# Stacks of queries in two transfers, denominators in one, a margin for transfers in the plan, and another order of key tiles

## The chip, the core and the metric

The kernel runs on one core of a Trainium2 chip. Its engines work through queues of their own, in order, and wait for each other by semaphores: TensorE (PE, with its weight loads PEld), VectorE (DVE), ScalarE (ACT), GpSimd (POOL) and SyncE (SP), which here issues every DMA. The metric is the device time of one execution in microseconds; a kernel's time is the median of its runs.

## The reference

Input x is 2048 rows of 448 floats. After a layernorm, multi-query attention and a gated MLP run side by side, and both are added to x:

```python
x = A_x
xn = _layernorm(x, axis=-1)
q = (xn @ wq).reshape(B, S, 16, 28).transpose(0, 2, 1, 3)     # 16 heads
k, v = xn @ wk, xn @ wv                                        # one head of keys and values, 28 wide
p = softmax(einsum("bhqd,bkd->bhqk", q, k) * 28 ** -0.5)
attention = einsum("bhqk,bkd->bhqd", p, v).transpose(0, 2, 1, 3).reshape(B, S, 448) @ wo
mlp = (silu(xn @ w1) * (xn @ w3)) @ w2                         # 448 -> 1792 -> 448
out = x + attention + mlp
```

(The projections, the softmax and the sum are written out from the reference's functions.) Everything is float32.

## The kernel before

**Work.** Queries are taken in 4 chunks of 512 (`qc`), heads 16 per chunk, so there are 64 steps `h`, in the text called heads. Float32 products are made from rounded parts: an operand is split into a high part and a low rest, and high x high, high x low and low x high are summed.

**Attention of one head.** `stack_load(h)` loads the head's queries into a stack `qs` of 84 rows (28 each of high, low and high) from a DRAM copy `qd`; the keys `kst` have three blocks that answer them. `leads(h)` makes 16 score tiles `ld` (128 keys x 512 queries each), one matmul each; VectorE keeps a running maximum `mx` over them. Ten of the sixteen tiles are *kept*: ScalarE copies them, in pairs, to SBUF (`pa`); KEEP lists the first tile of each pair. Then VectorE folds the maximum over the keys into `nm`, SP stores it to DRAM (`md`), loads it into the 85th row of the stack (`qs<-md`) and loads it broadcast over 128 partitions (`mb`). `weights_of(h, kt)` makes the exponentials: for a kept pair GpSimd adds the (negated) maximum, `pa<-pa,mb`, and ScalarE takes the exponential; the six tiles that are not kept are scored again with the 85th row (`sc`) and ScalarE takes their exponential from PSUM into `pb`. `values(h, j)` sums the weights with the values into `av`, in groups of 16 matmul records that mix the first half of head h with the second half of head h-1. `pair_done` and `norm` collect four heads in `o`, send their denominators through DRAM (`l1`, `l2`), take reciprocals, load them broadcast to 32 rows a head (`lb`, four transfers), and VectorE multiplies (`o<-o,lb`); `out_project` multiplies with `wo`.

**MLP.** `gate_up` and `down` make the tiles `g`, `u` and `dn` of 14 blocks of 128 columns per chunk, spread among the heads as filler for TensorE. Their split weights are made in the first chunk, stored, and loaded again (`w<-w13s`, `w<-w2s`) in the others.

**The order.** Nothing runs in the order in which it is written. `Plan.op` records each instruction with a cost, a latency and a due time; `Plan.order()` then plays a list scheduler: at each moment each engine takes the ready instruction of least due time, if its buffers can be had (`can`, with the pools MOST and SPARE, and SOON, how far ahead of the first TensorE work left a buffer may be taken). What comes out is the fixed order of every queue. The due times come from T0, T, LEAD and SPAN:

```python
    def begin(h):
        return T0 + T / 2 * h
```

The numbers only set the order. On the chip each engine goes as fast as its waits allow.

Of the kernel before, what the change touches and what calls it, by code (L numbers as in the profile page):

```python
# [20 lines left out]
P = 128  # L21
TC = 512
NQ = S // TC
TT = TC // P
HG = 4
# [18 lines left out]
MDUE, MRUSH, MSTEP = 28.0, 8, 9.0  # L44
MEND = -6.37
RATE = 290.0
BACKLOG = 1306.01
BULK = ("w13", "w2", "x", "raw", "raw2", "acc")
SOON = {"pa": 15.0, "qs": 0, "acc": 12.7, "o": 0, "x": 28.7}
PAIRS = 36  # L50
PAGES = 96 - 2 * PAIRS
SLACK = 37.1
REST = 0.0
LOADING = 105.0
BANKS = 8
MOST = {"pa": 19, "x": 16, "acc": 4, "w13": 5, "w2": 6, "h": 4, "oh": 3, "wo": 3, "xt": 4, "xn": 4, "wq": 4,
        "qt": 5, "pb": 7, "raw": 5, "raw2": 1, "t": 2, "qs": 6, "m": 2, "mxt": 3, "mb": 3, "o": 2, "lb": 1,
        "xp": 14, "wr": 4, "kv": 3, "at": 5, "mi": 6, "av": 2, "qp": 4}
SPARE = {"x": 3, "acc": 4, "w13": 2, "w2": 3, "raw": 4, "raw2": 3, "qt": 0, "wo": 0, "qs": 2}

# [26 lines left out]
class Plan:  # L87
# [40 lines left out]
    def order(self):  # L128
# [23 lines left out]

        def can(o):
# [143 lines left out]
def build(ctx, tc, x, wq, wk, wv, wo, w1, w3, w2, out):  # L297
# [39 lines left out]
    def dma(size, fn, **k):  # L337
        return plan.op("SP", 520.0, fn, size=size, **k)
# [170 lines left out]
    def project(qc, g, prio):  # L509
# [198 lines left out]
    def stack_load(h):  # L708
        q = stacks[h] = page("qs", f"qs{h}", F32R)
        plan.base = begin(h) - LEAD - SPAN - 8.0  # L710
        qc, lo = h // H, h % H * DH
        for b, src in enumerate((0, 1, 0)):
            dma(DH * TC * 4, lambda b=b, src=src: nc.sync.dma_start(
                f32(q.ap)[b * DH:(b + 1) * DH], qd[qc][src, lo:lo + DH]),
                reads=[qdb[qc, g] for g, (a, z) in enumerate(QROWS) if a < lo + DH and z > lo], parts=[q])

    def leads(h):

        mx, q = page("m", f"mx{h}"), stacks[h]
        last = None  # L720
        for kt in range(KT):
            plan.base = begin(h) - LEAD - SPAN + SPAN * kt / KT
            m = bank("at", f"ld{h}_{kt}")
            keep = kt in KEEP or kt - 1 in KEEP
            if kt in KEEP:
                p = pair("pa", f"pa{h}_{kt}")
            if keep:
                pt[h, kt] = p, int(kt not in KEEP)
            last = pe(512, lambda m=m, kt=kt: nc.tensor.matmul(  # L729
# [3 lines left out]
            if keep:  # L733
                act(512, lambda m=m, p=p, i=int(kt not in KEEP): nc.scalar.activation(p.ap[:, i], m.ap, AF.Copy),  # L734
                    reads=[m], parts=[p])
            if kt == 1:
                vec(512, lambda m=m, p=p: nc.vector.tensor_max(mx.ap, m.ap, p.ap[:, 0]), reads=[m], writes=[mx],
                    after=p.writers[:1], also=[p])
            elif kt:
                vec(512, lambda m=m: nc.vector.tensor_max(mx.ap, m.ap, mx.ap), reads=[m], writes=[mx])  # L740
# [27 lines left out]

    def weights_of(h, kt):


        plan.base = begin(h) + T * kt / KT
        if kt in KEEP:
# [14 lines left out]
    def values(h, j):  # L788


        todo = []
        for i in range(AVK):
            for g, kt in ((h, AVK * j + i), (h - 1, KT // 2 + AVK * j + i)):
                if 0 <= g < NH:
                    if g // 2 not in avb:
                        avb[g // 2] = bank("av", f"av{g // 2}")
                    todo.append((avb[g // 2], g, kt, *pt[g, kt]))

        def fn():
            for a, g, kt, p, i in todo:  # L800
                r = 64 * (kt % 2) + 32 * (g % 2)
                nc.tensor.matmul(a.ap[r:r + 32], vst_ap[:, kt], p.ap if i is None else p.ap[:, i], start=(kt < 2), stop=(kt >= KT - 2),  # L802
                                 skip_group_check=True)
        cost = AVK / 2 * 894.0 + 205.0
        plan.base = begin(h) + T * AVK * (j + 1) / KT + 1.5
        av_last[0] = plan.op("PE", cost, fn, lat=cost + 160.0,
                             reads=[p for *_, p, _ in todo] + [vst[kt // TT] for _, _, kt, _, _ in todo],
                             parts=[a for a, *_ in todo], after=[av_last[0]])

    def pair_done(u):  # L810
        w, half = divmod(u, 2)
        plan.base = begin(2 * u + 3) + 2.0
        if half == 0:
# [4 lines left out]
        vec(512, lambda: nc.vector.tensor_add(o.ap[r], a.ap[64:128], o.ap[r]), reads=[a], parts=[o],  # L818
            after=[c1])
        if half:  # L820
# [11 lines left out]
    def norm(w):  # L832
# [13 lines left out]
        lb = page("lb", f"lb{w}")  # L846
        for h in range(HG):
            dma(32 * TC * 4, lambda h=h: nc.sync.dma_start(
                lb.ap[32 * h:32 * h + 32], l2[h:h + 1].broadcast_to([32, TC])), reads=[l2b], parts=[lb])
        vec(512, lambda: nc.vector.tensor_mul(o.ap, o.ap, lb.ap), reads=[lb], writes=[o], cost=1000.0)  # L850
# [102 lines left out]
```

## Time and profile before

| | |
|---|---|
| median of 3 runs | 1169.39 us (1168.66 to 1171.07) |
| the profiled execution | 1164.6 us, span 1162.8 us |
| TensorE busy | 1130.5 us (97%), granted clock 0.996 |
| VectorE, ScalarE, GpSimd busy | 956.2, 961.4, 921.8 us |
| DMA queue | 101888 packets, 45.3% of the 16 engines' span |

A row of the page's groups gives line, engine, operation, out<-in, shape, count, busy time, mean of one, and the idle time before them with what ended it. A row of the waits gives who waited for whom, the total, the number and the longest. A piece of the chain gives start and length. `SPq` is SP's issuing.

### The profile page before, as it was taken

What the parts mean: (1) busy time and instruction counts of PE and PEld (TensorE: products, weight loads), DVE (VectorE), ACT (ScalarE), POOL (GpSimd) and SP (SyncE); (2) the same over time, 40 slices, a digit from 0 to 9 for tenths busy, and PEclk for the clock granted to TensorE, in tenths of its full rate; (3) what the DMA queues carried; (4) which work ended last, traced back from release to release, by engine and by line L of the source; (5) the groups of instructions that cost most, each with busy time, mean ns of one, the idle gap of its engine ahead of it and who ended that gap; (6) DMA issues with size and microseconds to landing.
All of it is one profiled execution on the core that took longest, in us unless ns stands there. A gap on an engine that the chain in (4) does not pass through costs nothing.

```text
span 1162.8 us, 18499 instructions
## 1 busy us (share of the span) xinstructions
PE 1130.5 (97%) x5810; PEld 742.1 (64%) x5810; DVE 956.2 (82%) x1798; ACT 961.4 (83%) x1599; POOL 921.8 (79%) x474
## 2 busy tenths in 40 slices
PE   6999999999999999999999999999999999999998
PEld 4876766565666666556666666566665666667664
DVE  7775688988798888888888888788898888898863
ACT  4546689999799988898899888898889888998873
POOL 4317899999688896888688878788788778988694
PEclk9999999999999999999999999999999999999998
DMA  7887874555513353232732551526243355143420
GB/s 201 274 300 246 279 244 140 186 191 187 180 47 103 102 195 117 89 120 68 237 127 65 160 183 33 152 60 194 67 171 101 109 165 172 62 132 108 145 61 32
DMA packets 101986, 168.68 MB, mean 145 GB/s; under 512 B 20980, under 2 KB 62644, under 8 KB 101888
## 3 DMA queue, kind: packets, MB, share of 16 engines
q1 hardware_dynamic: 101888, 167.50, 45.3%
q8 instruction: 46, 0.75, 0.3%
q14 instruction: 52, 0.43, 0.1%
HBM read 126.94 MB, written 39.83 MB: 143 GB/s over the span
## 4 chain that ended last, share of the span: by engine, by line
PE 52%; DVE 4%; ACT 3%; DMA 3%; issue 2%; POOL 1%; SPq 1%; DVEq 0%; ACTq 0%
PE av L802 13%; PE ld L729 12%; PE dn L361 7%; PE u L361 6%; PE g L361 6%; PE sc L782 5%; PE wo L361 3%; DVE mx L740 2%; DMA mb<-md 1%; ACT pa L734 1%; ACT pa L777 1%; DMA qs<-qd 1%; ACT pb L785 1%; POOL pa L775 1%; DMA lb<-l 1%
## 5 line engine op out<-in xcount | busy, mean ns | idle before, releaser
L775 POOL TENSOR_TENSOR pa<-pa,mb 128x1024 f32<-128x1024 f32 x320 | 761.8, 2412 | 107.3 <-DMA mb<-md 86.3
L740 DVE TENSOR_TENSOR mx<-ld,mx 128x512 f32<-128x512 f32 x896 | 583.0, 679 | 87.8 <-PE ld L729 64.0
L734 ACT ACTIVATE pa<-ld 128x512 f32<-128x512 f32 x640 | 369.0, 609 | 62.5 <-PE ld L729 53.4
L777 ACT ACTIVATE pa<-pa 128x1024 f32<-128x1024 f32 x320 | 343.5, 1077 | 30.3 <-POOL pa L775 30.1
L729 PE MATMUL ld<-qs,kst 84*128 84x512 f32 x1024 | 359.3, 409 | 9.0 <-DMA qs<-qd 3.1
L729 PEld LDWEIGHTS ld<-qs,kst 84*128 84x128 f32 x1024 | 188.3, 189 | 127.5 <-DVE mx L740 30.6
L785 ACT ACTIVATE pb<-sc 128x512 f32<-128x512 f32 x384 | 228.8, 611 | 27.1 <-PE sc L782 26.3
L802 PE MATMUL av<-pa,vst 128*32 128x512 f32 x1280 | 248.1, 600 | 0.3 <-DVE mx L740 0.2
L802 PE MATMUL av<-pb,vst 128*32 128x512 f32 x768 | 246.0, 596 | 0.0
L361 PE MATMUL dn<-w,h 128*128 128x448 f32 x672 | 171.1, 368 | 0.4 <-DVE o L818 0.3
L782 PE MATMUL sc<-qs,kst 85*128 85x512 f32 x384 | 154.6, 408 | 2.5 <-DVE acc L664 1.2
L361 PEld LDWEIGHTS dn<-w,h 128*128 128x128 f32 x672 | 126.1, 189 | 24.6 <-issue 5.5
L641 POOL TENSOR_TENSOR h<-t,h 128x512 fp32r<-128x512 f32 x56 | 72.6, 1296 | 54.9 <-ACT h L640 54.5
L802 PEld LDWEIGHTS av<-pa,vst 128*32 128x32 f32 x1280 | 51.5, 109 | 85.1 <-issue 71.6
L782 PEld LDWEIGHTS sc<-qs,kst 85*128 85x128 f32 x384 | 72.3, 188 | 41.5 <-issue 6.7
L802 PEld LDWEIGHTS av<-pb,vst 128*32 128x32 f32 x768 | 50.4, 109 | 38.6 <-issue 38.6
L664 DVE TENSOR_TENSOR acc<-dn,acc 128x448 f32<-128x448 f32 x80 | 48.8, 610 | 18.8 <-PE dn L361 18.3
L636 DVE SCALAR_TENSOR_TENSOR t<-u,t 128x512 f32<-128x512 f32 x56 | 38.2, 682 | 30.4 <-PE u L361 29.5
L361 PE MATMUL g<-x_0m,w 128*128 128x512 f32 x168 | 58.5, 398 | 0.3 <-DVE mx L740 0.3
L361 PE MATMUL u<-x_0m,w 128*128 128x512 f32 x168 | 56.4, 399 | 1.4 <-ACT pa L734 1.4
L361 PE MATMUL g<-x_2m,w 128*128 128x512 f32 x168 | 57.1, 402 | 0.0
L361 PE MATMUL u<-x_2m,w 128*128 128x512 f32 x168 | 54.6, 395 | 0.0
(84 smaller groups left out, 1186.8 us busy)
## 6 DMA issues: line engine op xcount, KB each, us to landing
w<-w13s SPq DMA_DIRECT2D x84, 512.0 KB
w<-w2s SPq DMA_DIRECT2D x42, 448.0 KB
mb<-md SPq DMA_DIRECT2D x64, 256.0 KB
w13s<-w SPq DMA_DIRECT2D x28, 512.0 KB
qs<-qd SPq DMA_DIRECT2D x192, 56.0 KB
wo<-wos SPq DMA_DIRECT2D x16, 448.0 KB
w2s<-w SPq DMA_DIRECT2D x14, 448.0 KB
raw<-w SPq DMA_DIRECT2D x28, 192.0 KB
```

Of the source, the lines that this page charges most:

```text
L361: nc.tensor.matmul(dst.ap[0:n, 0:width], lv(lb), rv(rb), start=(i == 0), stop=(i == len(terms) - 1))
L636: vec(512, lambda: nc.vector.scalar_tensor_tensor(t.ap, u.ap, 0.5, t.ap, op0=ALU.mult, op1=ALU.mult), reads=[u], writes=[t], prio=2 * half)
L641: gps(512, lambda: nc.gpsimd.tensor_sub(hl.ap, t.ap, f32(hh.ap)), reads=[t, hh], writes=[hl], prio=2 * half)
L664: vec(448, lambda: nc.vector.tensor_add(a.ap[:, 0:D], o.ap[:, 0:D], a.ap[:, 0:D]), reads=[o, a], prio=1.0))
L729: last = pe(512, lambda m=m, kt=kt: nc.tensor.matmul(m.ap, kst_ap[0:KS, kt * P:(kt + 1) * P], q.ap[0:KS], start=True, stop=True), reads=[q ...
L734: act(512, lambda m=m, p=p, i=int(kt not in KEEP): nc.scalar.activation(p.ap[:, i], m.ap, AF.Copy), reads=[m], parts=[p])
L740: vec(512, lambda m=m: nc.vector.tensor_max(mx.ap, m.ap, mx.ap), reads=[m], writes=[mx])
L775: gps(1024, lambda: nc.gpsimd.tensor_add(p.ap, p.ap, b.ap.unsqueeze(1).broadcast_to([P, 2, TC])), reads=[b], writes=[p], prio=-3.0)
L777: act(1024, lambda: nc.scalar.activation(p.ap, p.ap, AF.Exp, scale=SCALE), psum=False, writes=[p], prio=-1.0, after=[sqrt_last])
L782: pe(512, lambda: nc.tensor.matmul(o.ap, kst_ap[0:KS + 1, kt * P:(kt + 1) * P], q.ap[0:KS + 1], start=True, stop=True), reads=[q, kst[kt / ...
L785: act(512, lambda: nc.scalar.activation(p.ap, o.ap, AF.Exp, scale=SCALE), reads=[o], writes=[p], prio=0.0, after=[sqrt_last])
L802: nc.tensor.matmul(a.ap[r:r + 32], vst_ap[:, kt], p.ap if i is None else p.ap[:, i], start=(kt < 2), stop=(kt >= KT - 2), skip_group_check ...
```

## The change

It has these parts.

- **Stack of queries.** `stack_load` makes the rows high, high, low instead of high, low, high, so that the first two blocks are one transfer with a source that repeats (56 rows), and the third one more: two transfers instead of three. The keys' blocks become high, low, high.
- **Denominators.** `norm` loads `lb` with one transfer of 128 rows, the source 4 heads x 32 repeats, instead of four.
- **Key tiles.** KEEP, the order of the scores (SEEN) and of the weights (ORDER) change: the kept pairs are now (2,3), (5,6), (8,9), (11,12), (14,15); the unkept tiles 0, 1, 4 and 7 come early among the scores, and the places of kept and unkept tiles among the weights are the same as before.
- **Planner.** Each transfer counts 500 ns more (LATE); SLACK goes from 37.1 to 48.27 ns; TensorE may take an instruction whose buffers lie further ahead than SOON allows, if it has nothing else and 5 buffers stay free (EARLY); the costs of `values` and of the addition in `pair_done` are set anew; the other numbers move a little.

```diff
-KEEP = (0, 3, 6, 9, 12)
+KEEP = (2, 5, 8, 11, 14)
+SEEN = (2, 0, 1, 4, 5, 6, 7, 3, 8, 9, 10, 11, 12, 13, 14, 15)
+ORDER = (2, 3, 0, 5, 6, 1, 8, 9, 4, 11, 12, 7, 14, 15, 10, 13)
-T0, T, LEAD, SPAN = 70.94, 33.0, 9.2, 34.39
+T0, T, LEAD, SPAN = 69.04, 33.24, 8.59, 34.39
-QDUE, QSTEP = 34.79, 10.87
+QDUE, QSTEP = 38.84, 10.78
-XSTORE = 27.4, 13.8
+XSTORE = 32.5, 15.1
+LATE = 500.0
+EARLY = 5
-SLACK = 37.1
+SLACK = 48.27
...
-            if any(o.prio > head() + SOON.get(c, 40.0) for c in cats):
+            if early:
+                if any(len(p) - k < EARLY for k, p in zip(need[:2], pools) if k):
+                    return False
+            elif any(o.prio > head() + SOON.get(c, 40.0) for c in cats):
                 return False
...
+                    if best is None and e == "PE":
+                        best = min((o for o in ready[e] if locked(o, now) <= now and can(o, True)),
+                                   key=lambda o: (o.prio, o.n), default=None)
...
-                        lat = max(dma - now, o.size / 120.0) + 2000.0
+                        lat = max(dma - now, o.size / 120.0) + 2000.0 + LATE
...
-            for b, src in enumerate((qh, qh, ql)):
+            for b, src in enumerate((qh, ql, qh)):
...
-        for b, src in enumerate((0, 1, 0)):
-            dma(DH * TC * 4, lambda b=b, src=src: nc.sync.dma_start(
-                f32(q.ap)[b * DH:(b + 1) * DH], qd[qc][src, lo:lo + DH]),
-                reads=[qdb[qc, g] for g, (a, z) in enumerate(QROWS) if a < lo + DH and z > lo], parts=[q])
+        k = dict(reads=[qdb[qc, g] for g, (a, z) in enumerate(QROWS) if a < lo + DH and z > lo], parts=[q])
+        dma(2 * DH * TC * 4, lambda: nc.sync.dma_start(
+            f32(q.ap)[0:2 * DH], qd[qc][0:1, lo:lo + DH].broadcast_to([2, DH, TC])), **k)
+        dma(DH * TC * 4, lambda: nc.sync.dma_start(f32(q.ap)[2 * DH:KS], qd[qc][1, lo:lo + DH]), **k)
...
-        for kt in range(KT):
-            plan.base = begin(h) - LEAD - SPAN + SPAN * kt / KT
+        for n, kt in enumerate(SEEN):
+            plan.base = begin(h) - LEAD - SPAN + SPAN * n / KT
...
+        kt = ORDER[i]
+        plan.base = begin(h) + T * i / KT
...
-        cost = AVK / 2 * 894.0 + 205.0
+        cost = AVK / 2 * 858.0 + 300.0
...
-        for h in range(HG):
-            dma(32 * TC * 4, lambda h=h: nc.sync.dma_start(
-                lb.ap[32 * h:32 * h + 32], l2[h:h + 1].broadcast_to([32, TC])), reads=[l2b], parts=[lb])
+        dma(P * TC * 4, lambda: nc.sync.dma_start(lb.ap, l2.unsqueeze(1).broadcast_to([HG, 32, TC])),
+            reads=[l2b], parts=[lb])
```

What this does to the queues, at three places (numbers after a name's last underscore are buffer numbers; lines of the changed kernel stand about ten further down). First SP's queue, where head 31's maxima go out (`md31`, then `qs31<-md31` and the broadcast `mb31`) while a later head's stack, `qs34`, is loaded; `wo6` are output weights, `w132_...` and `w22_...` MLP weights. Before:

```order
L828 DMA wo6_6970<-wos_102 128x2x448
L762 DMA md31_176<-nm1_88 16x32
L713 DMA qs34_7068<-qd2_97 28x512 x3
L765 DMA qs31_6516<-md31_176 1x512
L767 DMA mb31_7083<-md31_176 128x512
L762 DMA md32_177<-nm0_87 16x32
L713 DMA qs35_7225<-qd2_97 28x512 x3
```

After:

```order
L839 DMA wo6_6927<-wos_102 128x2x448
L772 DMA md31_176<-nm1_88 16x32
L723 DMA qs34_7009<-qd2_97 56x1x512
L725 DMA qs34_7009<-qd2_97 28x512
L775 DMA qs31_6482<-md31_176 1x512
L777 DMA mb31_7036<-md31_176 128x512
L611 DMA w132_4_1_7042<-w13s4_1_112 128x1024
L772 DMA md32_177<-nm0_87 16x32
```

The stack still stands between `md31` and `mb31`, now as two transfers of 56 and 28 rows instead of three of 28; head 35's stack has moved behind `mb32`. Of the 64 heads, 24 have a stack directly behind their `md` in both orders.

Second the same queue where the denominators of group 7 go out (`l1`), come back spread over partitions (`lc1`), go out as reciprocals (`l2`) and are loaded broadcast (`lb7`). Before:

```order
L838 DMA l1_7_223<-o7_7114 4x512
L840 DMA lc1_94<-l1_7_223 128x16
L618 DMA w22_4_7505<-w2s4_135 128x2x448
L843 DMA l2_7_224<-lc1_94 128x16
L601 DMA w132_5_0_7520<-w13s5_0_113 128x1024
L848 DMA lb7_7546<-l2_7_224 32x512 x2
L762 DMA md34_179<-nm0_87 16x32
L848 DMA lb7_7546<-l2_7_224 32x512 x2
L601 DMA w132_5_1_7576<-w13s5_1_114 128x1024
L765 DMA qs34_7068<-md34_179 1x512
L767 DMA mb34_7583<-md34_179 128x512
```

After:

```order
L849 DMA l1_7_223<-o7_7051 4x512
L851 DMA lc1_94<-l1_7_223 128x16
L854 DMA l2_7_224<-lc1_94 128x16
L611 DMA w132_5_0_7494<-w13s5_0_113 128x1024
L772 DMA md34_179<-nm0_87 16x32
L858 DMA lb7_7516<-l2_7_224 128x1x512
L611 DMA w132_5_1_7526<-w13s5_1_114 128x1024
L775 DMA qs34_7009<-md34_179 1x512
L777 DMA mb34_7545<-md34_179 128x512
```

The four loads of `lb7`, split in two by `md34`, are one, behind `md34`.

Third TensorE's queue where head 24's scores begin (`ld24_<key tile>`), between those of head 23, scores with the 85th row of heads 20 and 21 (`sc`), and the MLP's `u` and `dn`. Before:

```order
L729 MATMUL ld24_0_5335<-qs24_5287,kst_74 128x512
L782 MATMUL sc20_11_5341<-qs20_4539,kst_74 128x512
L361 MATMUL u23_5272<-x1_0m_2777,w131_9_1_5053 128x512 x2
L729 MATMUL ld23_8_5348<-qs23_5098,kst_74 128x512
L361 MATMUL u23_5272<-x1_4m_3003,w131_9_1_5053 128x512
L729 MATMUL ld24_1_5353<-qs24_5287,kst_74 128x512
L361 MATMUL dn1_6_0_5357<-w21_6_4579,h20_4739 128x448
L729 MATMUL ld23_9_5361<-qs23_5098,kst_74 128x512
L361 MATMUL dn1_6_0_5357<-w21_6_4579,h20_4739 128x448
L729 MATMUL ld24_2_5366<-qs24_5287,kst_74 128x512
```

After:

```order
L739 MATMUL ld24_2_5308<-qs24_5241,kst_74 128x512
L371 MATMUL dn1_6_0_5297<-w21_7_4886,h21_5020 128x448
L739 MATMUL ld23_8_5312<-qs23_5055,kst_74 128x512
L739 MATMUL ld24_0_5317<-qs24_5241,kst_74 128x512
L371 MATMUL dn1_6_0_5297<-w21_8_4946,h22_5250 128x448 x2
L739 MATMUL ld23_9_5324<-qs23_5055,kst_74 128x512
L371 MATMUL dn1_6_0_5297<-w21_8_4946,h22_5250 128x448
L793 MATMUL sc21_1_5328<-qs21_4825,kst_74 128x512
L739 MATMUL ld24_1_5333<-qs24_5241,kst_74 128x512
```

The tiles of head 24 now come as 2, 0, 1 instead of 0, 1, 2. Over the program TensorE has the same 4785 matmuls (the profile has 5810, since each `av` and one other is recorded twice). Counted there, runs of `ld` and `sc` that follow each other without another matmul are 253 of one and 159 of four and more before, 358 and 136 after; and between a head's last `ld` and the first `av` that reads its weights stand 94 matmuls before and 101 after (medians of the 64 heads).

More of the change, by code (lines that the diff above doesn't have):

```diff
@@ L47 @@
 BACKLOG = 1306.01
+LATE = 500.0
+EARLY = 5
 BULK = ("w13", "w2", "x", "raw", "raw2", "acc")
-SOON = {"pa": 15.0, "qs": 0, "acc": 12.7, "o": 0, "x": 28.7}
+SOON = {"pa": 24.4, "qs": 0, "acc": 12.7, "o": 12.0, "x": 18.4}
 PAIRS = 36
 PAGES = 96 - 2 * PAIRS
-SLACK = 37.1
-REST = 0.0
+SLACK = 48.27
+REST = 4.41
 LOADING = 105.0
 BANKS = 8
[L56 to L59, printed above, removed]
+MOST = {"pa": 19, "x": 16, "acc": 4, "w13": 5, "w2": 6, "h": 4, "oh": 3, "wo": 3, "xt": 5, "xn": 4, "wq": 4,
+        "qt": 4, "pb": 7, "raw": 5, "raw2": 1, "t": 2, "qs": 7, "m": 2, "mxt": 3, "mb": 2, "o": 2, "lb": 1,
+        "xp": 14, "wr": 3, "kv": 3, "at": 5, "mi": 6, "av": 2, "qp": 4}
+SPARE = {"x": 3, "acc": 4, "w13": 2, "w2": 3, "raw": 4, "raw2": 2, "qt": 0, "wo": 0, "qs": 2}
 class Buf:
@@ L151, in head, with can @@
             return line[0][0] if line else 1e9
-        def can(o):
+        def can(o, early=False):
             need = [0, 0, 0]
@@ L720, in leads @@
         last = None
-        for kt in range(KT):
-            plan.base = begin(h) - LEAD - SPAN + SPAN * kt / KT
+        for n, kt in enumerate(SEEN):
+            plan.base = begin(h) - LEAD - SPAN + SPAN * n / KT
             m = bank("at", f"ld{h}_{kt}")
             keep = kt in KEEP or kt - 1 in KEEP
-            if kt in KEEP:
-                p = pair("pa", f"pa{h}_{kt}")
             if keep:
-                pt[h, kt] = p, int(kt not in KEEP)
+                i = int(kt not in KEEP)
+                p = pt[h, kt - 1][0] if i else pair("pa", f"pa{h}_{kt}")
+                pt[h, kt] = p, i
             last = pe(512, lambda m=m, kt=kt: nc.tensor.matmul(
@@ L767, in leads, with weights_of @@
         dma(P * TC * 4, lambda: nc.sync.dma_start(b.ap, md[h].broadcast_to([P, TC])), reads=[d], writes=[b])
-    def weights_of(h, kt):
-        plan.base = begin(h) + T * kt / KT
+    def weights_of(h, i):
+        kt = ORDER[i]
+        plan.base = begin(h) + T * i / KT
         if kt in KEEP:
@@ L792, in values @@
         for i in range(AVK):
-            for g, kt in ((h, AVK * j + i), (h - 1, KT // 2 + AVK * j + i)):
+            for g, n in ((h, AVK * j + i), (h - 1, KT // 2 + AVK * j + i)):
                 if 0 <= g < NH:
@@ L796, in values @@
                         avb[g // 2] = bank("av", f"av{g // 2}")
-                    todo.append((avb[g // 2], g, kt, *pt[g, kt]))
+                    todo.append((avb[g // 2], g, n, *pt[g, ORDER[n]]))
         def fn():
-            for a, g, kt, p, i in todo:
-                r = 64 * (kt % 2) + 32 * (g % 2)
-                nc.tensor.matmul(a.ap[r:r + 32], vst_ap[:, kt], p.ap if i is None else p.ap[:, i], start=(kt < 2), stop=(kt >= KT - 2),
+            for a, g, n, p, i in todo:
+                r = 64 * (n % 2) + 32 * (g % 2)
+                nc.tensor.matmul(a.ap[r:r + 32], vst_ap[:, ORDER[n]], p.ap if i is None else p.ap[:, i], start=(n < 2), stop=(n >= KT - 2),
                                  skip_group_check=True)
-        cost = AVK / 2 * 894.0 + 205.0
+        cost = AVK / 2 * 858.0 + 300.0
         plan.base = begin(h) + T * AVK * (j + 1) / KT + 1.5
         av_last[0] = plan.op("PE", cost, fn, lat=cost + 160.0,
-                             reads=[p for *_, p, _ in todo] + [vst[kt // TT] for _, _, kt, _, _ in todo],
+                             reads=[p for *_, p, _ in todo] + [vst[ORDER[n] // TT] for _, _, n, _, _ in todo],
                              parts=[a for a, *_ in todo], after=[av_last[0]])
@@ L818, in pair_done @@
         vec(512, lambda: nc.vector.tensor_add(o.ap[r], a.ap[64:128], o.ap[r]), reads=[a], parts=[o],
-            after=[c1])
+            after=[c1], cost=725.0)
         if half:
```

6 lines of the change are left out of this document (3 added, 3 removed).

## The prediction

> **What bounds the kernel now.** I read the page first (busy times, chain), then three stretches, the waits, and then pieces of the chain at places where TensorE lost time.
>
> ```profile
> span 1162.8 us, 18499 instructions
> PE 1130.5 (97%) x5810; PEld 742.1 (64%) x5810; DVE 956.2 (82%) x1798; ACT 961.4 (83%) x1599; POOL 921.8 (79%) x474
> PE 52%; DVE 4%; ACT 3%; DMA 3%; issue 2%; POOL 1%; SPq 1%; DVEq 0%; ACTq 0%
> ...
> L729 PE MATMUL ld<-qs,kst 84*128 84x512 f32 x1024 | 359.3, 409 | 9.0 <-DMA qs<-qd 3.1
> L802 PE MATMUL av<-pa,vst 128*32 128x512 f32 x1280 | 248.1, 600 | 0.3 <-DVE mx L740 0.2
> L782 PE MATMUL sc<-qs,kst 85*128 85x512 f32 x384 | 154.6, 408 | 2.5 <-DVE acc L664 1.2
> ```
>
> TensorE is busy for 97% of the span and carries 52% of the chain; the other three are near 80%. The change leaves every matmul in place, so only what TensorE loses to waits can move. The stretches say how much that is (columns: length, PE busy, PEld, DVE, ACT, POOL, granted clock, DMA share, GB/s):
>
> ```profile
> 0.00:39.00 39.00, 28.05 (x136) 21.77 (x137) 30.47 (x69) 17.66 (x35) 18.49 (x31) 1.00 0.76 222
> 39.00:1131.00 1092.00, 1075.89 (x5554) 704.77 (x5553) 913.42 (x1709) 930.49 (x1544) 888.59 (x435) 1.00 0.46 146
> 1131.00:1162.80 31.80, 26.58 (x124) 15.60 (x122) 12.33 (x22) 13.20 (x22) 14.76 (x10) 0.91 0.08 30
> ```
>
> Idle at the start: 39.00 - 28.05 = 11.0 us; at the end 31.80 - 26.58 = 5.2 us; in the middle, where the change works, 1092.00 - 1075.89 = 16.1 us. Some loss hides in "busy", since a matmul that waits behind its weights looks long:
>
> ```profile
> L729 PE MATMUL ld<-qs,kst x1024: 387/397/605, 46.7 to 1116.3; 84*128 84x512 f32 x171
> L782 PE MATMUL sc<-qs,kst x384: 389/397/505, 94.3 to 1142.7; 85*128 85x512 f32 x192
> ```
>
> Mean less median, (409 - 397) x 1024 + (408 - 397) x 384 ns = 12.3 + 4.2 = 16.5 us. So I count 16.1 + 16.5 = 32.6 us as what a better order could win in the middle. Who ends those waits (us in total, times, longest):
>
> ```profile
> PEld ld L729 <- DVE mx L740: 30.6, 54, 1.4
> PEld ld L729 <- ACT pa L734: 14.6, 20, 1.8
> ...
> POOL pa L775 <- DMA mb<-md: 86.3, 29, 9.8
> ACT pa L777 <- POOL pa L775: 30.1, 36, 3.1
> PE ld L729 <- DMA qs<-qd: 3.1, 4, 1.5
> SPq L762 <- DVE nm L760: 377.0, 59, 13.7
> ```
>
> A score matmul mostly waits for its PSUM bank, which VectorE (maximum) or ScalarE (copy) frees. Those are late because they stand in order behind something that waits. One such place, from the chain (start, length):
>
> ```profile
> 902.71 0.40 SPq L713
> ...
> 903.20 0.53 SPq L618
> ...
> 903.78 0.58 SPq L713
> ...
> 904.72 6.30 DMA mb<-md
> 911.09 4.77 POOL pa L775 x2
> 915.88 1.06 ACT pa L777
> 916.94 0.49 ACT pa L734
> ```
>
> The broadcast of the maxima (mb) lands 6.30 us after its issue, which itself stood behind two stack transfers and a weight load; GpSimd waits for it, ScalarE's exponential waits for GpSimd, and the copy that would free a bank stands behind the exponential. Two more kinds of place:
>
> ```profile
> 857.62 2.96 DMA lb<-l
> ...
> 860.77 2.65 DVE o L850
> ...
> 867.51 2.54 PE u L361 x10
> ```
>
> ```profile
> 727.19 5.29 DMA qs<-qd
> ```
>
> In the first, the product with the denominators (L850) holds VectorE up, and TensorE then runs ten matmuls in 2.54 us; in the second a head's first score waits for its stack.
>
> **The change, part by part.** The sum is made against the profiled execution, 1164.6 us (span 1162.8 and 1.8 around it); the median of the runs shown is 1169.39, 4.8 us above, and I carry differences over to it.
>
> *Order of key tiles and the planner's margins.* In the order of TensorE's instructions, between the last score of a head (ld) and its first weighted sum (av) there stood 94 matmuls (median of 64 heads), now 101; the least was 79, now 86. At the chain's 2.54 us for ten, 0.25 each, the path maximum, md, mb, GpSimd, exponential gets 7 x 0.25 = 1.8 us more room in each head. GpSimd's wait for mb was 86.3 / 29 = 3.0 us where there was one; 1.8 / 3.0 = 60% of it is covered. Of the named TensorE waits, 14.6 of 45.2 us end with a ScalarE copy: 32% of 32.6 us is 10.5 us, and of that I take two thirds as rooted in GpSimd, because the exponential's wait for it (30.1 us) is twice what the copies then cost TensorE (14.6): 0.60 x 7.0 = -4.2 us. Bounds: 0, if the room lies in front of something else that is late, and -6.3 us, if all of the ScalarE part is of this kind.
>
> ```profile
> L740 DVE TENSOR_TENSOR mx<-ld,mx 128x512 f32<-128x512 f32 x896 | 583.0, 679 | 87.8 <-PE ld L729 64.0 <-ACT pa L734 12.1 <-DVE mx L740 0.5
> L713 SPq DMA_DIRECT2D qs<-qd x192: 306/382/1087, 41.7 to 1082.7; - x192
> L848 SPq DMA_DIRECT2D lb<-l x60: 308/413/1286, 210.9 to 1112.8; - x60
> q1 hardware_dynamic: 101888, 167.50, 45.3%
> ```
>
> *Finer alternation.* Counting ld and sc matmuls that follow each other directly, runs of four and more fall from 159 to 136 (-14%) and singles rise from 253 to 358. Short runs ask less of VectorE, whose maximum takes 679 ns against 0.25 us of the matmul that feeds it. The VectorE part of the loss is 68% of 32.6 = 22 us; 14% of it is -3.1 us. Bounds: 0 and, if the waits sit only in the long runs, twice that, -6.2 us. The permission to start work early (EARLY) only fills holes of the plan and is in this count.
>
> *Fewer transfers.* SP issues 64 stack loads fewer at 0.38 us and 15 x 3 denominators at 0.41: 24.5 + 18.6 = 43 us of SP. SP sits 377 us waiting for maxima, so that is cover, not gain, except where a stack load stands between md and mb: 24 heads before and 24 after. There mb is issued 0.38 us sooner; 24 x 0.38 = 9 us of GpSimd's wait, of which by the ratio above (4.2 of 86.3) TensorE sees 0.4 us. Against it: no row shows how one transfer of 56 rows is carried. Bounds from the queue's row: a packet takes 0.453 x 16 x 1162.8 us / 101888 = 83 ns. On all 16 engines a stack's rows cost 4 packets, 0.3 us; on two engines 28 packets, 2.3 us. A head's first score would then come between 0.4 us sooner and 2.0 - 0.4 = 1.6 us later. I take +0.6 us, nearest the middle: the four heads that wait now wait 2.4 us more and perhaps as many again join, +2.4. Likewise lb, 128 rows: three issues fewer (-1.24 us) against 32 packets on four engines instead of 8 (24 x 83 ns = +2.0 us), so -1.2 to +0.8 us each; 15 of them on VectorE, taken as 0. Range of both: -4 to +14 us.
>
> By the Trainium skill, "DMA: Bandwidth & Descriptors", "Why a DMA increments its semaphore by 16 and not by 1", the number of engines is the largest up to 16 that divides the slowest dimension of both sides: here the source starts with 2 copies (stack) or 4 heads (denominators). By that the stack's term is the far bound, 1.6 us a head, and the sum is some 8 us worse than the one I take; the trace of before agrees only in that nothing there contradicts it. "Rules for kernel authors" on that page warns of a leading broadcast in so many words.
>
> *The rest.* The keys' blocks (high, low, high) that answer the new stack, and the later projections and stores (QDUE, XSTORE) move work that feeds heads long after; TensorE's first rows stay, so the 11.0 us at the start stay, and so does the end (5.2 us): the last normalisation is not touched. Cost 0, between -2 and +2. SP's rows of md move with the heads: the wait of 377 us is its cover.
>
> Sum: -4.2 - 3.1 - 0.4 + 2.4 = -5.3. 1164.6 - 5.3 = 1159.3 us for the profile, 1169.4 - 5.3 = 1164.1 us for the median.
>
> **Rivals.**
> *Few engines (slower).* The stack's 112 KB and the denominators sit on two and four engines. Each stack lands 1.6 us later, and in the 24 heads where it stands between md and mb, the broadcast queues behind it on those engines. For it: no row excludes it. Against: the plan counts 0.5 us more for every transfer (LATE), and a stack is asked for 8 us ahead of its scores, while the one quoted took 5.29. Price: the 4 waiting heads (3.1 us) become 12 at 1.0 us, +9; mb later by 0.75 us in 24 heads (a third of the 2.3, since the two overlap), 18 us of GpSimd's wait, a third on TensorE's path, +6; less 4 won by the order: +11, 1180 us. It decides once more than about eight heads wait for their stack.
>
> *Waits only change places.* VectorE, ScalarE and GpSimd keep their 956, 961 and 922 us; a bank freed sooner in one place is freed later in another. The distance between uses of one PSUM bank is as before in the order (for ld a median of 16 matmuls, before and after), which speaks for it. 1169 us.
>
> *Half of all middle waits go.* 32.6 / 2 = 16: 1153 us. For it: the roots (mb, lb, qs) are few and each is touched. Against: 54 small waits for VectorE, at most 1.4 us each, are no single mechanism.
>
> **Numbers.** The forecast (between 1158 and 1167) has 0.48, few engines 0.22, places changed 0.18, half of all 0.12. Faster by over 0.2% (2.3 us, about what a measurement of this kernel tells from no change): 0.48 + 0.12 = 0.60; within 0.2%: 0.18; slower 0.22. The range reaches to the rivals on both sides without their far tails: 1152 to 1180.
>
> **What would show it.** PE busy plus idle: middle idle under 14 us, start and end as before. GpSimd's wait for mb well under 86 us, ScalarE's for GpSimd under 25. The means of ld and sc nearer to 397 ns. If the few engines are real, the wait of ld for qs grows from 3.1 us to over 8, pieces of the chain "DMA qs" and "DMA mb" get longer, and the DMA share stays while landings come later. The prediction is wrong if the stack waits eat what the order wins, or if VectorE's 30.6 us do not fall.

## The result, and the profile after

The changed kernel takes 1227.07 us (median of 6 runs, 1223.4 to 1234.44) against 1170.89 us for the kernel before in the same comparison: 1.0486 times as long, 95% interval 1.0446 to 1.0526, or 56 us slower. The prediction was 1164.1 us with a range up to 1180, so the sign was wrong and the range missed by 47 us. The profiled execution has a span of 1221.6 us (1162.8 before).

From the page of the changed kernel, busy times and the two groups of score matmuls (`ld` is now L739, `sc` L793), then the three stretches with the same columns as before:

```profile
span 1221.6 us, 18354 instructions
...
PE 1154.8 (95%) x5810; PEld 753.9 (62%) x5810; DVE 954.6 (78%) x1798; ACT 964.3 (79%) x1599; POOL 919.6 (75%) x474
...
L739 PE MATMUL ld<-qs,kst 84*128 84x512 f32 x1024 | 361.6, 414 | 14.8 <-DMA qs<-qd 11.9
...
L793 PE MATMUL sc<-qs,kst 85*128 85x512 f32 x384 | 157.1, 416 | 21.2 <-DMA qs<-md 17.0
```

```profile
0.00:39.00 39.00, 24.67 (x117) 19.30 (x117) 27.07 (x64) 15.42 (x28) 18.06 (x30) 0.99 0.75 219
39.00:1189.80 1150.80, 1103.52 (x5576) 720.17 (x5574) 915.18 (x1713) 934.54 (x1549) 884.28 (x433) 0.98 0.44 138
1189.80:1221.60 31.80, 26.61 (x123) 14.43 (x119) 12.32 (x21) 14.36 (x23) 17.30 (x12) 0.96 0.08 29
```

TensorE's idle time is 14.3 us at the start (11.0 before), 47.3 us in the middle (16.1) and 5.2 us at the end (5.2). Of the 58.8 us that the span grew, 3.3 + 31.2 are idle time that the profile shows as such, and 24.3 are in "busy" (1154.80 less 1130.52). Counted from start to start of neighbouring matmuls, what lies above the usual distance is 119.8 us after and 65.5 before, 54 of the 58.8 us. VectorE, ScalarE and GpSimd have the same work as before.

Most of the growth in "busy" goes with TensorE's granted clock. In the clock rows of the trace it stands at 0.50 in ten stretches of 3.4 to 10.2 us, 55.6 us in all; before there were two, 11.4 us in all. Matmuls that follow each other there without idle time take some 20.0 us more than at their usual distance, against 2.5 before, so about 17.5 of the 24.3 us. One stretch, behind a wait of `sc` for 3.1 us (columns: length, PE busy, granted clock, DMA share, GB/s):

```profile
905.80:909.70 3.90, 3.90 (x20) 1.00 0.92 182
909.70:912.80 3.10, 0.03 (x1) 0.87 1.04 291
912.80:918.60 5.80, 5.77 (x14) 0.50 0.24 88
```

From 912.8 to 918.6 us a matmul of `ld` takes 628 ns instead of 397, and the next one starts after 0.43 us instead of 0.23. Eight of the ten stretches lie in the middle. Each begins during an idle time of TensorE of 1.6 to 5.1 us or at most 1.5 us behind it; two of these idle times end with the stack, three with the one row `qs<-md`, three with VectorE. The medians of `ld` and `sc` do not show this (397 and 398 ns), because few of their matmuls fall into such stretches; the means rose from 409 and 408 to 414 and 416 ns. That the waits bring on the lower clock is read from the order of events; no run changes the clock alone.

The waits (total us, times, longest) say which waits grew:

```profile
POOL pa L786 <- DMA mb<-md: 118.7, 36, 10.5
...
PEld ld L739 <- DVE mx L750: 38.2, 55, 1.6
...
ACT pa L788 <- POOL pa L786: 23.2, 26, 2.5
...
DVE o L860 <- DMA lb<-l: 21.5, 10, 4.8
PEld sc L793 <- DVE mx L750: 20.9, 27, 3.5
PE sc L793 <- DMA qs<-md: 17.0, 11, 3.6
...
PE ld L739 <- DMA qs<-qd: 11.9, 9, 3.7
```

Three waits for transfers stand here that hardly existed before. `ld` waits for the stack (3.1 us in 4 places, now 11.9 in 9). VectorE waits for the denominators (0.4 us, now 21.5). The third was not in the prediction: `sc`, the scores with the 85th row, wait 17.0 us for `qs<-md`, the load of that one row, which the change does not touch; before, no such wait is listed.

```profile
PEld sc L782 <- DVE mx L740: 5.4, 14, 0.9
...
DVE o L850 <- DMA lb<-l: 0.4, 1, 0.4
```

These two lines are of the kernel before; the first is used further down. One of the 11 places where `sc` waits for its row, in the timeline of SyncE's queue (start, length, line) and then in the chain:

```profile
902.50 0.57 SPq L858 DMA_DIRECT2D lb<-l  x1
903.17 0.63 SPq L723 DMA_DIRECT2D qs<-qd  x1
903.85 0.44 SPq L725 DMA_DIRECT2D qs<-qd  x1
904.35 0.24 SPq L775 DMA_DIRECT2D qs<-md  x1
904.68 0.34 SPq L777 DMA_DIRECT2D mb<-md  x1
```

```profile
904.35 8.35 DMA qs<-md
912.70 0.14 issue
912.83 1.19 PE sc L793 x2
```

One row of 2 KB took 8.35 us from issue to landing, behind a merged `lb` and a merged stack. In the completion records the two engines of the merged stack end at 912.13 and 912.99 us, the row in between at 912.70; of the 28 rows issued behind the 56 the first engine ends at 906.76 and the last at 913.18. Other transfers were under way too: the DMA share was 0.92 from 905.8 to 909.7 us. Over the 64 heads the trace's completion records give this, from issue to landing (us, median and 90%):

| transfer | before | after |
|---|---|---|
| `qs<-md`, one row | 1.44, 2.84 | 3.44, 5.04 |
| whole stack, from its first issue | 4.72, 8.26 | 6.47, 8.50 |
| `mb<-md`, 128 rows | 3.66, 5.30 | 4.38, 6.14 |
| `lb<-l`, all four heads, from the first issue | 5.01, 5.36 | 6.11, 8.48 |
| records at the end of a 28-row stack transfer / the 56-row one / `lb` / one row | 15 / - / 16 / 2 | 15 / 3 / 5 / 2 |

The last row reads as the number of engines and one more, wherever that is under 16: 14 engines for 28 rows, two for the merged 56 rows, four for the merged denominators, one for one row. The one more comes first: at the place above 0.4 to 1.1 us after the start of the issue, 2 us and more ahead of the rest. The counts of engines follow the rule of the Trainium skill, "DMA: Bandwidth & Descriptors", "Why a DMA increments its semaphore by 16 and not by 1", which the prediction cited, and this trace agrees with it. The number of packets says the same. Before it was 101888, now it is

```profile
q1 hardware_dynamic: 99324, 167.49, 44.1%
```

The 2564 packets fewer are all of 4 bytes, and 64 x (3 x 14 - 14 - 2) + 15 x (4 x 16 - 4) = 2564: one such packet for each engine of a transfer, with the counts of the table.

### The profile page after: what moved, and what is told of

It reads as the page before. It is cut to its first block, busy times and chain, and to the rows that moved or that the text cites. A ratio compares the mean times of both kernels' runs of the same rounds, so it can differ in the third digit from the quotient of the medians.

```text
span 1221.6 us, 18354 instructions
## 1 busy us (share of the span) xinstructions
PE 1154.8 (95%) x5810; PEld 753.9 (62%) x5810; DVE 954.6 (78%) x1798; ACT 964.3 (79%) x1599; POOL 919.6 (75%) x474
## 5 line engine op out<-in xcount | busy, mean ns | idle before, releaser
L739 PE MATMUL ld<-qs,kst 84*128 84x512 f32 x1024 | 361.6, 414 | 14.8 <-DMA qs<-qd 11.9
L788 ACT ACTIVATE pa<-pa 128x1024 f32<-128x1024 f32 x320 | 343.6, 1079 | 23.5 <-POOL pa L786 23.2
L739 PEld LDWEIGHTS ld<-qs,kst 84*128 84x128 f32 x1024 | 190.1, 192 | 138.0 <-DVE mx L750 38.2
L796 ACT ACTIVATE pb<-sc 128x512 f32<-128x512 f32 x384 | 231.7, 616 | 41.6 <-PE sc L793 40.2
L813 PE MATMUL av<-pb,vst 128*32 128x512 f32 x768 | 248.6, 602 | 0.0
L371 PE MATMUL dn<-w,h 128*128 128x448 f32 x672 | 180.6, 377 | 8.1 <-DVE acc L674 7.2
L793 PE MATMUL sc<-qs,kst 85*128 85x512 f32 x384 | 157.1, 416 | 21.2 <-DMA qs<-md 17.0
L371 PEld LDWEIGHTS dn<-w,h 128*128 128x128 f32 x672 | 129.2, 194 | 39.1 <-issue 10.5
L793 PEld LDWEIGHTS sc<-qs,kst 85*128 85x128 f32 x384 | 73.4, 192 | 62.3 <-DVE mx L750 20.9
L371 PE MATMUL u<-x_0m,w 128*128 128x512 f32 x168 | 59.1, 409 | 2.3 <-DVE mx L750 2.1
L747 DVE TENSOR_TENSOR mx<-ld,pa 128x512 f32<-128x512 f32 x64 | 43.7, 682 | 13.5 <-ACT pa L744 7.8
```

What stands on the lines that cost most here:

```text
L371: nc.tensor.matmul(dst.ap[0:n, 0:width], lv(lb), rv(rb), start=(i == 0), stop=(i == len(terms) - 1))
L739: last = pe(512, lambda m=m, kt=kt: nc.tensor.matmul(m.ap, kst_ap[0:KS, kt * P:(kt + 1) * P], q.ap[0:KS], start=True, stop=True), reads=[q ...
L788: act(1024, lambda: nc.scalar.activation(p.ap, p.ap, AF.Exp, scale=SCALE), psum=False, writes=[p], prio=-1.0, after=[sqrt_last])
L793: pe(512, lambda: nc.tensor.matmul(o.ap, kst_ap[0:KS + 1, kt * P:(kt + 1) * P], q.ap[0:KS + 1], start=True, stop=True), reads=[q, kst[kt / ...
L796: act(512, lambda: nc.scalar.activation(p.ap, o.ap, AF.Exp, scale=SCALE), reads=[o], writes=[p], prio=0.0, after=[sqrt_last])
L813: nc.tensor.matmul(a.ap[r:r + 32], vst_ap[:, ORDER[n]], p.ap if i is None else p.ap[:, i], start=(n < 2), stop=(n >= KT - 2), skip_group_c ...
```

## The experiments

**Which part costs the time.** Four kernels: the changed kernel with the stack's first transfer issued as two of 28 rows, in the same place of the queue (the plan and every engine's order stay as in the changed kernel); the same with the denominators as four; with both; and the kernel before with only the stack's 56 rows merged.

```diff
 stack_three, against the changed kernel:
-        dma(2 * DH * TC * 4, lambda: nc.sync.dma_start(
-            f32(q.ap)[0:2 * DH], qd[qc][0:1, lo:lo + DH].broadcast_to([2, DH, TC])), **k)
+        def twice():
+            for b in range(2):
+                nc.sync.dma_start(f32(q.ap)[b * DH:(b + 1) * DH], qd[qc][0, lo:lo + DH])
+        dma(2 * DH * TC * 4, twice, **k)
```

> The changed kernel in its own order, but the 56 rows of a stack go out as two transfers of 28 rows, one behind the other, in the place of the one. Few engines (the merged stack lands late because two DMA engines carry it, and the one-row load of the maxima queues behind it on one of them): most of the loss goes, 1227 -> 1175 to 1185 us; the waits of sc for qs<-md (17.0 us) and of ld for qs<-qd (11.9 us) fall below 3 and 5 us. New order (the order of key tiles and the planner's numbers are what costs): no change worth naming, 1220 to 1228 us. Denominators (the merged load of lb is the cause): 1225 us.

Measured: 1182.46 us, ratio 1.0091 (1.0074 to 1.0109). The one-row load lands in 1.42 us again (median). The wait of `sc` for it falls to 5.5 us only, not below 3 as expected; the merged denominators are still there.

```diff
 lb_four, against the changed kernel:
-        dma(P * TC * 4, lambda: nc.sync.dma_start(lb.ap, l2.unsqueeze(1).broadcast_to([HG, 32, TC])), ...
+        def each():
+            for h in range(HG):
+                nc.sync.dma_start(lb.ap[32 * h:32 * h + 32], l2[h:h + 1].broadcast_to([32, TC]))
+        dma(P * TC * 4, each, reads=[l2b], parts=[lb])
```

> The changed kernel in its own order, but the denominators go out as four transfers of 32 rows in the place of the one of 128. Few engines, with the stack as the main part: 1227 -> 1215 to 1224 us, and VectorE's wait of o for lb falls from 21.5 us to under 5. Denominators as the main part: under 1200 us. New order: 1227 us, since TensorE never waits for lb itself.

Measured: 1209.01 us, 1.032 (1.0298 to 1.0342), faster than the 1215 to 1224 expected: with the stack still merged, the merged denominators cost 18 us. The two kernels separate the waits. First the one with merged denominators and split stack, then the one with merged stack and split denominators:

```profile
DVE o L862 <- DMA lb<-l: 16.3, 11, 2.8
...
PE sc L795 <- DMA qs<-md: 5.5, 7, 1.6
...
PE ld L741 <- DMA qs<-qd: 0.4, 1, 0.4
```

```profile
PE ld L739 <- DMA qs<-qd: 14.0, 8, 4.4
...
PE sc L793 <- DMA qs<-md: 11.7, 11, 2.2
...
DVE o L862 <- DMA lb<-l: 4.3, 4, 1.3
```

VectorE's wait for the denominators goes with the merged `lb`; TensorE's waits for the stack and, for the larger part, for the one row go with the merged stack.

> The changed kernel in its own order with both old ways of loading (three and four transfers); against the kernel before it leaves the new order and margins alone. Few engines: 1160 to 1172 us, so the order by itself is worth -10 to +1 us; the prediction's own terms for the order (-4.2 and -3.1 us) say 1163 us. New order: 1210 us or more.

Measured (both edits together): 1172.83 us, 1.0012 (1.0001 to 1.0023), just above the range expected and 10 us above the 1163 of the prediction's own terms. With both transfers split nothing measurable is left of the loss, and nothing of a gain: the new order and margins are worth nothing here. Against this version, the merged denominators cost 0.8% (9 us), the merged stack 3.1% (36 us), both 4.7% (55 us), some 10 us more than the two apart.

```diff
 before_stack_two, against the kernel before:
+        def part(b):
+            if b == 0:
+                nc.sync.dma_start(f32(q.ap)[0:2 * DH], qd[qc][0:1, lo:lo + DH].broadcast_to([2, DH, TC]))
+            elif b == 1:
+                nc.sync.dma_start(f32(q.ap)[2 * DH:KS], qd[qc][1, lo:lo + DH])
...
-            for b, src in enumerate((qh, qh, ql)):
+            for b, src in enumerate((qh, ql, qh)):
```

> The kernel before in its own order, but a stack goes out as one transfer of 56 rows (high twice) and one of 28 (low), at the places of its first two transfers; the third place is empty, and the keys' blocks follow (high, low, high). Few engines: slower by 30 to 55 us, 1200 to 1225 us, with the plan's margin of 0.5 us absent. New order: 1165 to 1172 us, since 64 issues of SP are saved and nothing is moved.

Measured: 1202.61 us, 1.0262 (1.0235 to 1.029). In the old order, with the old plan, the merged stack alone loses 31 us, by the same waits (and with seven stretches at a clock of 0.50, 35.9 us in all, where the matmuls lose 11.4 us against 2.5 before):

```profile
PE ld L733 <- DMA qs<-qd: 16.7, 10, 5.1
...
PE sc L786 <- DMA qs<-md: 12.2, 13, 2.3
```

**Merging, or the number of engines?** The same 56 rows in one transfer of the same bytes, but with the two copies of a row next to each other in the stack (the rows of the keys follow), so that the outer dimension of the source is 28 and not 2:

```diff
 interleaved, against the changed kernel with lb as in lb_four:
-            f32(q.ap)[0:2 * DH], qd[qc][0:1, lo:lo + DH].broadcast_to([2, DH, TC])), **k)
+            f32(q.ap)[0:2 * DH], qd[qc][0, lo:lo + DH].unsqueeze(1).broadcast_to([DH, 2, TC])), **k)
...
-                    f32(kst_ap)[b * DH:(b + 1) * DH, qc * TC:(qc + 1) * TC], f32(src.ap)[0:DH]),
+                    f32(kst_ap)[b:2 * DH:2, qc * TC:(qc + 1) * TC] if b < 2 else
+                    f32(kst_ap)[2 * DH:KS, qc * TC:(qc + 1) * TC], f32(src.ap)[0:DH]),
```

> The changed kernel with the stack's 56 rows still in one transfer of the same bytes, from the same source rows and at the same place, but with the two copies of a row next to each other (row 2d and 2d+1 of the stack are dimension d, so the source's outer dimension is 28 instead of 2), the key rows in that order too, and the denominators in four transfers. Theory A (the loss comes from the count of engines that carry a transfer: two with an outer dimension of 2): the transfer ends with 15 updates instead of 3, the queries' one-row load lands in about 1.4 us again (3.4 after), and the time is that of the version with both transfers split, within 0.5%: 1168 to 1178 us. Theory B (a transfer of 56 rows is bad as such: bigger, twice the packets behind one semaphore): the one-row load stays above 2.5 us and the time stays 2% or more above before, 1195 to 1215.

Measured: 1172.26 us, 1.0023 (1.0001 to 1.0044). The transfer ends with 15 records instead of 3, the one row lands in 1.46 us (median), the wait of `sc` for it is not listed any more, and the wait of `ld` for the stack is 0.5 us in one place.

> The kernel before, its order of the work unchanged, with the first place of the stack bringing all 56 rows in one transfer with the copies of a row next to each other, the second the other 28 rows and the third none (64 issues of SyncE fewer). The only difference to the version that took 1.0262 of the time before is the order of the rows in the stack. Theory A (count of engines): 0.996 to 1.003 of the time before; what the merge can win by itself, SyncE's issues, is then seen undisturbed. Theory B (merging as such): 1.02 to 1.03 again.

Measured (the same rows in the kernel before, its order unchanged, the stack in 56 + 28): 1172.68 us, 1.002 (1.0 to 1.0041). The one difference to the version above that took 1.0262 is the order of the rows within the transfer (and of the keys' rows that answer them). Bytes and data packets are the same; only the 4-byte packets differ, 100992 packets in all against 100224, which is 768 = 64 x 12, fourteen engines instead of two for each of the 64 transfers. So it is the count of engines. It also shows that fewer issues are not less time for issuing: SyncE's rows for the stack, in the interleaved version and in the changed kernel (min/median/max in ns), against 382 for one of three before:

```profile
L724 SPq DMA_DIRECT2D qs<-qd x64: 801/848/1717, 42.0 to 1087.8; - x64
L726 SPq DMA_DIRECT2D qs<-qd x64: 393/541/1117, 42.8 to 1088.7; - x64
```

```profile
L723 SPq DMA_DIRECT2D qs<-qd x64: 609/652/1079, 42.6 to 1139.4; - x64
L725 SPq DMA_DIRECT2D qs<-qd x64: 339/443/1228, 43.3 to 1140.1; - x64
```

A stack cost SyncE 3 x 382 = 1146 ns before, 652 + 443 = 1095 ns merged and 848 + 541 = 1389 ns interleaved: the issue of a merged transfer is longer.

**Is it the stack's own lateness, or what the two engines hold up?** The version with both split, and per head one more transfer of 56 rows from the same source into memory that nobody reads or waits for, once with the outer dimension 2, once with 28:

```diff
 ghost_two, against both_split (ghost_fourteen: unsqueeze(1), broadcast_to([DH, 2, TC])):
         def twice():
+            nc.sync.dma_start(spare[h % 8], qd[qc][0:1, lo:lo + DH].broadcast_to([2, DH, TC]))
             for b in range(2):
```

> The version with both transfers split, and per head, ahead of the stack, one more transfer of 56 rows from the same source, with an outer dimension of 2, into spare memory that nobody reads or waits for. The stack itself comes on 14 engines. It tells apart the two ways in which a transfer on two engines may cost time. Theory C (the two engines' backlog holds up what comes behind, the one-row load of the queries above all): the one-row load lands in about 3 us, PE waits for it as in the changed kernel (10 us or more in all), and the time is 1190 to 1215 us. Theory D (only the stack's own lateness costs): the one-row load may be late, but the time stays within 0.7% of the version with both split, 1170 to 1181.

Measured: 1209.89 us, 1.0337 (1.0294 to 1.0381).

> The same additional transfer with the same bytes, but with an outer dimension of 28 (14 engines): the control for the one before. Both theories expect 1172 to 1182 us, since its 56 packets of some 83 ns are 4 to each of 14 engines, 0.3 us; if it costs as much as the transfer on two engines, the bytes or SyncE's issue cost the time and not the few engines.

Measured: 1180.17 us, 1.0079 (1.0055 to 1.0102). GpSimd's and TensorE's waits, first with the transfer that nobody waits for on two engines, then with the same bytes on fourteen:

```profile
POOL pa L791 <- DMA mb<-md: 117.2, 38, 10.5
...
PE sc L798 <- DMA qs<-md: 10.0, 12, 2.0
...
PE ld L744 <- DMA qs<-qd: 9.4, 9, 2.0
```

```profile
POOL pa L791 <- DMA mb<-md: 110.0, 40, 8.3
...
PE ld L744 <- DMA qs<-qd: 1.6, 1, 1.6
...
PE sc L798 <- DMA qs<-md: 1.6, 3, 0.7
```

The bytes and the issue cost 0.7% over the version without them (1.0079 against 1.0012). The transfer on two engines costs another 2.6%, 30 us, though nobody waits for what it carries: the backlog holds up what comes behind. The one row lands in 2.82 us instead of 1.46 (medians). A stack transfer on fourteen engines lands in 4.94 instead of 2.26 us, so it needs at least one of these two as well. The 30 us are near the 36 us that the merged stack costs in this order. The pair differs in more than the count of engines, though: the trace has the transfer on two engines as two packets of 57344 bytes (median 2.84 us each), the control as 56 packets of 2 KB, while the merged stack itself goes in packets of 2 KB. So this pair shows that a backlog on two engines is enough to cost such a time; that the merged stack makes it by its count of engines is shown by the interleaved versions. How the 30 us divide between the row, the stack and `mb` stays open, since all three are late for the same reason.

**Where the order's gain went.** The plan's numbers alone, with before's key tiles and transfers; and the new order of the key tiles alone, with before's numbers and both transfers split:

```diff
 margins_only, against the kernel before (with all other new numbers of the plan, buffer limits too):
-T0, T, LEAD, SPAN = 70.94, 33.0, 9.2, 34.39
+T0, T, LEAD, SPAN = 69.04, 33.24, 8.59, 34.39
...
+LATE = 500.0
+EARLY = 5
 tiles_only, against both_split: the same lines the other way, LATE 0, no early start
```

> The kernel before (its transfers, its order of key tiles) with the plan's new numbers alone: due times, page limits, half a microsecond more for each transfer, the permission to start early. By its order TensorE has 99 matmuls (median) between a head's last score and its first weighted sum (94 before, 101 with the tiles too), and 140 runs of four and more scores (159 before, 136 with both). Theory E (room in TensorE's order is handed back elsewhere, since the other engines keep their work and move with the scores): 0.998 to 1.003 of the time before, GpSimd's wait for mb again 80 to 100 us. Theory F (one of the two parts gains what my prediction said, and the other loses it again): this part is the one with most of the room, so 0.993 to 0.997.

> The changed kernel with both transfers split, with the plan's numbers of before: only the order of the key tiles is new (96 matmuls of room, 147 runs of four and more scores). Theory E: 0.998 to 1.004 of the time before. Theory F: 1.003 to 1.008, since it would have to give back what the margins win.

Measured: margins alone 1173.15 us, 1.0021 (1.0002 to 1.004); tiles alone 1170.62 us, 0.9988 (0.997 to 1.0006). Neither part holds a gain that the other gives back. The waits, margins first, then tiles, then both together:

```profile
POOL pa L783 <- DMA mb<-md: 83.3, 34, 12.5
...
PEld ld L737 <- DVE mx L748: 32.9, 61, 1.4
...
PEld sc L790 <- DVE mx L748: 13.2, 26, 0.8
...
PEld ld L737 <- ACT pa L742: 8.4, 18, 0.9
```

```profile
POOL pa L788 <- DMA mb<-md: 120.6, 38, 12.0
...
PEld ld L741 <- DVE mx L752: 32.8, 55, 2.0
...
PEld ld L741 <- ACT pa L746: 18.0, 28, 1.1
...
PEld sc L795 <- DVE mx L752: 7.6, 19, 0.8
```

```profile
POOL pa L788 <- DMA mb<-md: 97.3, 38, 9.5
...
PEld ld L741 <- DVE mx L752: 32.8, 55, 0.8
...
PEld sc L795 <- DVE mx L752: 13.1, 26, 0.8
...
PEld ld L741 <- ACT pa L746: 7.1, 11, 1.8
```

What `ld` wins back of its waits for ScalarE's copies with the new margins (14.6 us before, 8.4 and 7.1), `sc` loses to VectorE's maxima (5.4 before, 13.2 and 13.1). And GpSimd's wait for `mb` goes from 83 to 121 us among three kernels whose times lie within 0.4%: it is no measure of TensorE's time. None of these versions beats the kernel before by more than the measurement can tell.

## Why the prediction was wrong, step by step

- **Fewer transfers (+2.4, taken).** This is the step that failed. The mechanism stood there as the far bound, and its first half was sized well against the old order: the whole stack lands 1.75 us later (bound: 1.6), and `ld` waits 11.9 us in 9 places where the rival said 12 heads at 1.0 us. With the order held it is more, 6.47 us against 3.79 with both split. Missing was what else uses those two engines, and what a wait costs besides its length. The prediction let a late stack delay only its own reader and, by a third, `mb`. It did not look at the one-row load `qs<-md`, which one engine carries and which is issued behind a stack that follows its `md` in 33 heads (24 of these stacks directly behind `md`); that put 17.0 us of new waits on TensorE itself. And behind its long waits TensorE ran at half the clock, some 17.5 us more than before, for which the sum has no term. Measured, the merged stack costs 31 us in the old order and 36 in the new one.
- **The choice of the middle.** Between -0.4 and +1.6 us a head the prediction took +0.6 "nearest the middle", with the rule of the Trainium skill ("DMA: Bandwidth & Descriptors", "Why a DMA increments its semaphore by 16 and not by 1") already pointing at the far bound. The trace of before spoke for it too, more than "nothing there contradicts it": its transfers of 28 rows, of one row and of 32 or 128 rows end with 15, 2 and 16 records. The far bound was the right one. Even so, "some 8 us worse" for it was too small, for the reason above.
- **Denominators (0, taken; bound +0.8 us each).** From the first issue to the last landing they took 5.01 us before and 6.11 after; with the order held, 4.35 (split) against 6.11. So +1.1 to +1.8 us each, and VectorE waited 21.5 us instead of 0.4. They cost 9 us with the stack split and 18 us with it merged. The bound came from 32 packets at the mean of 83 ns, with nothing ahead of them on the four engines.
- **SyncE's issues (-0.4).** The saving was taken as one issue less, 0.38 us a stack; it is 1146 - 1095 = 0.05 us. Nothing was won: interleaved it costs 0.24 us more of SyncE, and the time in the old order is 1.002.
- **Order of key tiles (-4.2).** Wrong in size, at its lower bound. The room of 7 matmuls, 1.8 us, is there in the version with both split (24.9 us from a head's last `ld` to its first `av` instead of 23.2, means), but half of it is eaten ahead of `mb`: from the end of the last `ld` to the landing of `mb` it is 0.90 us a head longer (`md` issued 0.48 later, `mb` 0.37 later behind `md`, its landing 0.05 longer, means of 64 heads in the two traces). The rest does not show in the time either, because the waits for VectorE grew, as the lines above show. The rival "waits only change places" describes this part; why `md` comes later was read from the traces and not tested.
- **Finer alternation (-3.1).** Wrong in direction: fewer long runs of scores (136 against 159), and more waiting for VectorE, not less (`ld` 32.8 against 30.6 us, `sc` 13.1 against 5.4, with both split).
- **The rest (0, start and end unchanged).** The end stayed at 5.2 us. The start did not: 14.3 us of idle time against 11.0 (12.3 with both split).
- **The signs to look for.** Those of the few engines came true in part: `ld` waited over 8 us for the stack (11.9), and the DMA share did not rise (0.44 against 0.46) while landings came later. The pieces of the chain that were named did not grow: the longest for the stack has 5.23 us against 5.29 and for `mb` 6.23 against 6.30. New among the long pieces are those for the one row, 4.29 to 8.35 us. Of the signs of a gain one came true in a slower kernel: ScalarE's wait for GpSimd fell under 25 us (23.2). And what it named as showing it wrong, that VectorE's 30.6 us do not fall, is what happened (38.2).
- **A reading.** The 52% of TensorE in the chain are a share of the span, and the chain shown reaches back only to 397 us (after: 879 us), so it says nothing of the time ahead of that. The sum does not use it.
- **The rival "few engines"** had the right sign and the right transfers, with 0.22 and 1180 us; it lacked the one-row load, a cost of the denominators and the time at half the clock. Even its end of the range was 47 us short.

## What to carry to other kernels

Before two transfers become one, write down the outer dimension of both sides and count the engines that it leaves: here 2 instead of 28 cost 2.6% in the old order, and the same bytes with the copies next to each other (outer dimension 28) cost nothing that can be told from no change. Price a transfer on few engines by what is issued behind it, a one-row load above all, and not only by its own reader. Count a long wait of the busiest engine at more than its length if the trace shows a lower clock behind such waits, as here. Room made in the order of one engine is a gain only if the work that it should cover does not itself start later; look at that path's first step before counting the room.

## What the runs showed of the hardware that was not expected

- A 2 KB load that one engine carries waited behind a transfer on two engines: 3.44 us in the median instead of 1.44, while the mean busy share of the 16 engines was 0.44. At the worst it took 8.35 us, at a place where that share was 0.92.
- The mean of 83 ns a packet, which the prediction used, is over packets from 4 bytes to 4 KB. Those of 2 KB took 84 ns in the median and 109 in the mean before, 84 and 114 in the changed kernel. So 28 of them one after another on one engine are 2.4 to 3.2 us, an estimate.
- The time of an issue on SyncE depends on the transfer's shape: medians of 382 ns for 28 rows, 652 for 2 x 28 and 848 for 28 x 2 of the same bytes, 567 for 4 x 32 against 413 for 32.
- The granted clock of the changed kernel's profile was 0.978, against 0.996 before and 0.991 to 0.997 in the five versions within 0.3% of the time before. The difference is made of short stretches at 0.50 behind idle times of TensorE, and at 0.50 a `ld` took 628 ns instead of 397. Not every idle time of that length was followed by one: in the kernel before with the merged stack, idle times of 2.2, 1.9 and 1.8 us were not.
